# Output projection of a linear-attention + MLP block: seven block products for blocks 0 and 1 in one pair of output chunks, accumulators loaded by chunks into attention's tiles

## Chip, cores, metric

One core of one Trainium2 chip. The metric is the device time of the whole kernel in microseconds, lower is better.

## The reference: what is computed

Cut to what matters (S = 2048 tokens, D = 640 features, 32 heads of 20, MLP width 1728, all float32):

```python
xn = _layernorm(x)
out = x + attention(xn) + mlp(xn)
# attention: qkv = xn @ wqkv; phi = softmax features of q and k, per head
#            o = phi_q (phi_k^T v) / (phi_q (phi_k^T 1));  result = o @ wo
# mlp:       gelu(layernorm(xn) @ w1 + b1) @ w2 + b2
```

The change touches only the last product, `o @ wo` (2048x640 by 640x640), and what is added to it.

## The kernel before

Everything is kept transposed: features lie on the 128 partitions, tokens on the free axis. The 2048 tokens are four blocks b of 512; the 640 features are five chunks c or m of 128. A float32 matrix product is made exact enough by splitting both operands into a high part (rounded, `F32R`) and the rest, and by adding three matmuls (`mm3`, lines 69 to 72: high by high, high by low, low by high). So one output tile (128 features by 512 tokens) of the projection takes 5 chunks by 3 = 15 matmuls of 128x512.

The order of time: queries, keys and values; then the MLP of blocks 0 and 1 is done (its sums wait in DRAM as `a0` and `a1`); then the MLP of blocks 2 and 3 runs on TensorE, with attention (class `Attention`) beside it; last comes the output projection, which this case is about.

Before the projection, attention leaves its quotient in `ob`, one tile of five chunks for each block. `split` turns it into high parts `oh` (ScalarE) and low parts `ol` (VectorE) in the token order that the matmuls want. For block 3 the reciprocals `rx` come last: VectorE spreads them over partitions (`stream_shuffle`, line 1263) and GpSimd multiplies (line 1265), chunk by chunk, while the projection of the earlier blocks is already running.

The projection before:

- Blocks 0 and 1: ten calls of `column`, one for each block and output chunk m: 15 matmuls into PSUM bank 6 or 7 in turn, then VectorE adds the bank to the accumulator (line 1481) and SyncE stores the result.
- Blocks 2 and 3, output chunks 0 to 3 (two pairs, k = 0 and 1): seven block products in place of eight (Strassen-Winograd over pairs of input chunks, pairs of output chunks and the two token blocks). `product` makes 6 matmuls; `rest` adds the fifth input chunk (3 matmuls); `read` (line 1518) is VectorE adding a PSUM bank to an accumulator. Banks are named a, b and c; a bank is read in the middle and accumulated further, so the next product in it waits for that read. Output chunk 4 of both blocks is a `column` as before.
- The combined operands. Sums of the weights: loaded by `load_sums`, added on GpSimd by `add` (line 1424), split by `hi_sum` on ScalarE (line 1427) and by `lo_sum` on VectorE (line 1431). Differences of the attention outputs: `combine` on GpSimd (line 1440), `turn_hi` on ScalarE (line 1456, once into SBUF and once into a PSUM bank, bank 3 or 4 in turn), `turn_lo` on VectorE (line 1461). There are eight of these (i = 1 to 4, q = 0 and 1).

What sets the order: TensorE, VectorE, ScalarE and GpSimd run the order in which the program is written, each strictly in turn. The steps beside the matmuls are hung on ticks: `mlp.tick()` is called once per group of three matmuls in the program, and the list `steps` says at which tick each step is issued. So a step's place in VectorE's queue is fixed by hand, relative to the reads of PSUM banks that TensorE waits for. The order of SyncE's DMA queue is chosen by a scheduler.

The accumulators of blocks 0 and 1 come back from DRAM whole (1280 KB each, line 1290) into the tiles that held `ob` of these blocks.

Of the kernel before, what the change touches and what calls it, by code (L numbers as in the profile page):

```python
# [8 lines left out]
F32 = mybir.dt.float32  # L9
# [42 lines left out]
def tile_kernel(ctx: ExitStack, tc: tile.TileContext, x, xT, wkT, wqT, wv, wphi, wo, w1, b1, w2, b2,  # L52
# [1109 lines left out]
    class Attention:  # L1162

        def __init__(self, b, bank):
            self.b, self.n, self.bank = b, 0, bank
            self.ob = acc01.tile([P, KC, 512], F32, name=f"acc{b % 2}")
            self.ts = ep.tile([P, 512], F32, name="ts")
            self.t10 = ep.tile([42, 512], F32, name="t10")
            self.es = {}
# [101 lines left out]
        def split(self, c, eng):  # L1271

            b = self.b

            def tokens(ap):
                return ap.rearrange("p (q t n) -> p t q n", q=4, t=4)

            def parts(ap):
                return ap.rearrange("p (t q n) -> p t q n", q=4, t=4)

            if c == 0:
                self.oh, self.ol = (yp.tile([P, KC, 512], F32R, name=f"y{p}{b % 2}") for p in range(2))
            if c < KC:
                nc.scalar.activation(parts(self.oh[:, c, :]), tokens(self.ob[:, c, :]), AF.Copy)
            if c:
                eng.tensor_tensor(parts(self.ol[:, c - 1, :]), tokens(self.ob[:, c - 1, :]), f(parts(self.oh[:, c - 1, :])), op=ALU.subtract)
            if c == KC and b < 2:

                acc[b] = tfp.tile([P, KC, 512], F32, name=f"tf{b}")
                nc.sync.dma_start(acc[b], a_dram[b])  # L1290
# [10 lines left out]
    def first_split():  # L1301
        for c in range(KC + 1):
            at[0].split(c, nc.vector)
            if c % 2:
                yield
# [84 lines left out]

    w2t, parts = mlp.take_pair(6, True, 3)
    ws = pairs(w1t, w2t)
    for b in range(2, 4):
# [8 lines left out]
        else:  # L1402
            load_wo()
            mlp.beside = both(mlp.beside, first_split())
    finish(before)
    load_ob(1)

    sums, turned = [], {}

    def load_sums():  # L1410
        sums.append(wp.tile([P, 4, D], F32, name="w3").rearrange("p i d -> p (i d)")[:, :4 * 512])
        nc.sync.dma_start(sums[0].rearrange("p (c n) -> p c n", c=4), wo[:4 * P, :512].rearrange("(c p) n -> p c n", p=P))
        hi = wp.tile([P, 4, D], F32R, name="w1").rearrange("p i d -> p (i d)")
        lo = [bp.tile([P, 11, P], F32R, name="kvs").rearrange("p i d -> p (i d)"), rp.tile([P, 3, 2, P], F32R, name="s").rearrange("p i k n -> p (i k n)")]
        sums.extend([hi, lo])

    def lo_part(o):
        return sums[2][0][:, o:] if o < 5 * 256 else sums[2][1][:, o - 5 * 256:]

    def add(i):  # L1420

        (a11, a12), (a21, a22) = ([sums[0].rearrange("p (q r k j n) -> p q r k j n", q=2, r=2, k=2, j=2)[:, :, r, :, j] for r in range(2)] for j in range(2))
# [3 lines left out]
    def hi_sum(c):  # L1426
        nc.scalar.activation(sums[1][:, c * 512:c * 512 + 512], sums[0][:, c * 512:c * 512 + 512], AF.Copy)

    def lo_sum(o, w):
        at_ = slice(o, o + w)  # L1430
        nc.vector.tensor_tensor(lo_part(o)[:, :w], sums[0][:, at_], f(sums[1][:, at_]), op=ALU.subtract)

    def combine(i, q):

        c0, c1 = 2 * q, 2 * q + 1
        x = {(b, c): at[b].ob[:, c] for b in (2, 3) for c in (c0, c1)}
        t = {j: turned[j, q][0] for j in (1, 2, 3, 4) if (j, q) in turned}
        o = ep.tile([P, 512], F32, name="e", bufs=6) if i in (2, 3) else x[2, c0 if i == 1 else c1]
        x0, x1 = {1: lambda: (x[3, c0], x[2, c0]), 2: lambda: (x[3, c1], t[1]), 3: lambda: (x[3, c1], x[3, c0]), 4: lambda: (x[2, c1], t[2])}[i]()
        nc.gpsimd.tensor_tensor(o, x0, x1, op=ALU.subtract)  # L1440
        turned[i, q] = [o]
# [3 lines left out]
    def turn_hi(i, q):  # L1445

        src = turned[i, q][0].rearrange("p (q t n) -> p t q n", q=4, t=4)
        n = 2 * (i - 1) + q
        if n == 7:
            parts = [ep.tile([P, 512], F32, name="e", bufs=6).bitcast(F32R) for _ in range(2)]  # L1450
        else:
            m = mtile(n, F32R)
            parts = [m[:, p, :512] for p in range(2)]
# [3 lines left out]
        turned[i, q] += [bank, parts]  # L1457

    def turn_lo(i, q):
        _, bank, (hi, lo) = turned[i, q]  # L1460
# [3 lines left out]
    steps += [(12 + 2 * i, lambda i=i: add(i)) for i in range(4)]  # L1464
    steps += [(20 + c, lambda c=c: hi_sum(c)) for c in range(4)]
    steps += [(22 + n, lambda o=o, w=w: lo_sum(o, w)) for n, (o, w) in enumerate(((0, 512), (512, 512), (1024, 256), (1280, 256), (1536, 512)))]
    for n, (i, q) in enumerate((i, q) for i in (1, 2, 4, 3) for q in range(2)):
        steps += [(42 + 2 * n, lambda i=i, q=q: combine(i, q)), (45 + 2 * n, lambda i=i, q=q: turn_hi(i, q)), (46 + 2 * n, lambda i=i, q=q: turn_lo(i, q))]
    for n, t in ((1, 3), (2, 28), (3, 59)):
        steps += [(t + c, lambda n=n, c=c: at[n].split(c, nc.vector)) for c in range(KC + 1)]  # L1470
# [141 lines left out]
```

## Time and profile before

| | us |
|---|---|
| median of 3 runs | 711.22 (710.29 to 712.26) |
| the profiled execution, device time | 709.75 |
| its span, first to last instruction | 708.0 |
| PE busy / DVE / ACT / POOL in the span | 701.1 / 526.4 / 353.1 / 435.6 |
| the projection's first matmul | starts at 638.88 |
| its last matmul | starts at 704.33 |

PE is TensorE, DVE VectorE, ACT ScalarE, POOL GpSimd, SP SyncE. A row of a timeline gives the start in microseconds from the span's beginning, the time taken, the engine, the source line, the operation, written tile and read tiles, the shape, and how many instructions the row merges; a bracket at the end is the idle time before it and what ended it. A matmul row's time is its way through the array, and matmuls overlap: what one more matmul costs is the distance between two starts. In rows of grouped waits, the columns are: who waited, for whom, microseconds in total, how often, the longest.

### The profile page before, as it was taken

To read this page: it belongs to the slowest core of one execution; us is meant where nothing else is said; L and a number is where in the kernel's file an instruction comes from. 1 tells how busy PE (TensorE), PEld (TensorE's weight loads), DVE (VectorE), ACT (ScalarE), POOL (GpSimd) and SP (SyncE) were. 2 spreads that over 40 slices of the span, in tenths; PEclk is the share of its full clock that TensorE was granted. 3 is DMA by queue.
4 is the path that set the end of the run, shared out by engine and by line. 5 is a ranking of instruction groups with operands and counts; after the bars stand their busy time and mean duration, and the time that the engine had idled before them with its cause. 6 is when DMAs were issued, how large, how long until landed. Compare 5 with 4: busy or idle time off the path is not lost.

```text
span 708.0 us, 9794 instructions
## 1 busy us (share of the span) xinstructions
PE 701.1 (99%) x3369; PEld 590.3 (83%) x3369; DVE 526.4 (74%) x840; ACT 353.1 (50%) x583; POOL 435.6 (62%) x374
## 2 busy tenths in 40 slices
PE   9999999999999999999999999999999999999998
PEld 7788888888888888888888888878888878888886
DVE  7877755988745788788888878748678785696773
ACT  6434554444434545544444547457676757561250
POOL 3611314577245997898777979548688897462530
PEclk9999999999999999999999999999999999999999
DMA  9823642475621227336400708873355558537212
GB/s 328 287 74 113 190 122 98 156 263 174 219 105 74 94 75 231 86 97 200 114 0 15 177 0 316 227 215 126 109 160 172 164 166 276 216 124 262 91 60 104
DMA packets 66295, 107.61 MB, mean 152 GB/s; under 512 B 7478, under 2 KB 31830, under 8 KB 64366
## 3 DMA queue, kind: packets, MB, share of 16 engines
q1 hardware_dynamic: 65942, 106.98, 47.1%
q8 instruction: 26, 0.43, 0.2%
q14 instruction: 23, 0.19, 0.1%
q10 hardware_dynamic: 304, 0.01, 0.0%
HBM read 72.42 MB, written 34.55 MB: 151 GB/s over the span
## 4 chain that ended last, share of the span: by engine, by line
PE 93%; DVE 4%; ACT 1%; DMA 1%; issue 0%; ACTq 0%; DVEq 0%; SPq 0%
PE bank L906 28%; PE bank L70 18%; PE bank L72 18%; PE bank L71 18%; PE bank L976 3%; PE bank L646 2%; PE bank L1214 1%; PE bank L1215 1%; DVE st L138 1%; DMA e<-e 1%; PE bank L308 1%; PE bank L327 1%; PE bank L326 1%; PE bank L307 1%; PE bank L1146 1%
## 5 line engine op out<-in xcount | busy, mean ns | idle before, releaser
L906 PE MATMUL bank<-wkh,y 128*128 128x512 f32 (+1 forms) x480 | 139.6, 365 | 0.0
L64 POOL TENSOR_TENSOR w<-r,w 128x640 fp32r<-128x640 f32 x32 | 52.3, 1648 | 93.1 <-ACT w L61 57.7
L70 PE MATMUL bank<-m,w 128*128 128x512 f32 x274 | 108.0, 394 | 1.1 <-DVE acc L329 1.0
L71 PE MATMUL bank<-m,w 128*128 128x512 f32 x274 | 106.8, 390 | 0.0
L70 PE MATMUL bank<-y,w 128*128 128x512 f32 (+1 forms) x274 | 106.5, 389 | 0.0
L71 PE MATMUL bank<-y,w 128*128 128x512 f32 (+1 forms) x274 | 106.1, 387 | 0.0
L72 PE MATMUL bank<-y,w 128*128 128x512 f32 (+1 forms) x270 | 104.4, 387 | 0.0
L72 PE MATMUL bank<-m,w 128*128 128x512 f32 x262 | 102.1, 390 | 0.0
L906 PEld LDWEIGHTS bank<-wkh,y 128*128 128x128 f32 x480 | 87.6, 188 | 13.2
L906 PE MATMUL bank<-wkl,y 128*128 128x512 f32 (+1 forms) x240 | 87.4, 364 | 0.0
L942 ACT ACTIVATE m<-m,rs_all 128x1280 f32<-128x1280 f32 x32 | 43.7, 1365 | 42.9 <-POOL m L941 42.8
L70 PEld LDWEIGHTS bank<-m,w 128*128 128x128 f32 x274 | 51.5, 188 | 12.4 <-DVE acc L329 1.4
L70 PEld LDWEIGHTS bank<-y,w 128*128 128x128 f32 x274 | 51.5, 188 | 10.8 <-issue 0.4
L71 PEld LDWEIGHTS bank<-y,w 128*128 128x128 f32 x274 | 51.5, 188 | 10.5 <-DMA y<-t 0.4
L71 PEld LDWEIGHTS bank<-m,w 128*128 128x128 f32 x274 | 51.5, 188 | 10.4 <-DVE m L461 0.2
L72 PEld LDWEIGHTS bank<-y,w 128*128 128x128 f32 x270 | 50.8, 188 | 10.3
L944 DVE TENSOR_REDUCE sm<-m 128x64 f32<-128x1280 f32 x32 | 47.4, 1482 | 14.9 <-ACT m L942 14.8
L72 PEld LDWEIGHTS bank<-m,w 128*128 128x128 f32 x262 | 49.2, 188 | 10.3
L906 PE MATMUL bank<-w,y 128*128 128x512 f32 x240 | 57.4, 391 | 0.0
L941 POOL TENSOR_TENSOR m<-m,mx 128x640 f32<-128x640 f32 (+2 forms) x48 | 44.4, 938 | 19.3 <-DVE mx L930 19.3
L331 DVE TENSOR_TENSOR acc<-bank,acc 128x512 f32<-128x512 f32 x70 | 47.0, 684 | 11.0 <-PE bank L72 6.1
L64 DVE TENSOR_TENSOR m<-m,m 128x512 fp32r<-128x512 f32 (+1 forms) x34 | 27.9, 828 | 36.0 <-ACT m L61 36.0
(216 smaller groups left out, 1516.7 us busy)
## 6 DMA issues: line engine op xcount, KB each, us to landing
r<-in_w SPq DMA_DIRECT2D x52, 320.0 KB
e<-e SPq DMA_DIRECT2D x40, 256.0 KB
e<-acc SPq DMA_DIRECT2D x52, 160.0 KB
acc<-in_xT SPq DMA_DIRECT2D x4, 1280.0 KB
t<-t SPq DMA_DIRECT2D x8, 512.0 KB
tf<-t SPq DMA_DIRECT2D x2, 1536.0 KB
xb<-in_x SPq DMA_DIRECT2D x8, 320.0 KB
t<-in_x SPq DMA_DIRECT2D x8, 320.0 KB
```

The source lines that it names most:

```text
L64: eng.tensor_tensor(lo, src, f(hi), op=ALU.subtract)
L70: nc.tensor.matmul(ps, lh, rh, start=first, stop=False, **kw)
L71: nc.tensor.matmul(ps, lh, rl, start=False, stop=False, **kw)
L72: nc.tensor.matmul(ps, ll, rh, start=False, stop=last, **kw)
L138: nc.vector.bn_stats(st[:, i, h, :], xb[:, h * 320:(h + 1) * 320])
L331: nc.vector.tensor_tensor(acc[b][:, m, :], pw, acc[b][:, m, :], op=ALU.add)
L646: nc.tensor.matmul(ps[:, u * nh * DF:(u + 1) * nh * DF], raw[:nh * DH, u * P:(u + 1) * P], wpt[:nh * DH, g, :nh, 1:], start=True, stop=True)
L906: nc.tensor.matmul(ps, lh[:, kc, c], rh[:, kc], start=n == 0, stop=n == 3 * KC - 1)
L941: subs[n, t] = nc.gpsimd.tensor_tensor(ep[:, s], a, b, op=ALU.subtract)
L942: exps[n, t] = nc.scalar.activation(e, e, AF.Exp, scale=rs_all[:, t:t + 1])
L944: nc.vector.tensor_reduce(sm, e.rearrange("p s (h f) -> p (s h) f", f=DH), axis=AX, op=ALU.add)
L976: nc.tensor.matmul(kvp[g // 2][:, (g % 2) * 240:(g % 2) * 240 + 240].rearrange("p (s f) -> p s f", s=4), v[:, g * VS:(g + 1) * VS], ft[:, ...
```

## The change

In the projection of blocks 0 and 1 the output chunks 0, 1 and 4 stay `column`s (six of them). Chunks 2 and 3 (the pair k = 1) are now made with the seven block products too: `opened(0, 1)` and `closed(0, 1)`, which are the old loop bodies made into functions, and which are called one straight after the other. For blocks 2 and 3 the order stays: both `opened`, the column, both `closed`.

What comes with it:

- Eight more combined operands for blocks 0 and 1: `combine`, `turn_hi`, `turn_lo` with b0 = 0. They overwrite `ob` of these blocks. Those with i = 1 are written over chunks 0 and 2 of `oh` and `ol` of block 1.
- `ob` must live on, so the accumulators of blocks 0 and 1 come one chunk at a time (256 KB each) into attention's `e` tiles, `ts`, `t10`, `ph` and a part of `w3` (`load_a`, `load_sums`). They are queued before the projection begins.
- `split` is cut in two steps, and blocks 2 and 3 put their parts into the tiles of blocks 0 and 1, so each chunk's split waits until the last product that reads the old chunk is through.
- `lo_sum` is done for the pair k = 1 first (ticks 20 to 26), and for k = 0 late (ticks 56 to 62).
- The last operand's parts go into a tile `rx`.

```diff
-    for b in range(2):
-        for m in range(KC):
-            column(b, m, [6 + (b + m) % 2])
+    for n, (b, m) in enumerate((b, m) for b in range(2) for m in (0, 1, 4)):
+        column(b, m, [6 + n % 2])
+    opened(0, 1)
+    closed(0, 1)
     for k in range(2):
-        place("a", k, k)
...
+        opened(2, k)
     column(2, 4, [2])
     for k in range(2):
...
+        closed(2, k)
```

The two functions, which before stood in the loops with block 2 and 3 written in:

```diff
+    def opened(b0, k):
+        place("a", k, k)
+        product("a", k, "a11", "b11", b0, True)
+        read("a", k, 0, b0, False)
+        place("c", k, (2, 5)[k])
+        product("c", k, "a12", "b21", b0, True)
+        rest("c", k, 0, b0)
+        read("c", k, 0, b0)
+
+    def closed(b0, k):
+        place("b", k, (5, 2)[k])
+        product("b", k, "s1", "t1", b0, True)
+        read("b", k, 1, b0 + 1, False)
+        product("a", k, "s2", "t2", b0)
+        read("a", k, 0, b0 + 1, False)
+        place("c", k, (2, 5)[k])
+        product("c", k, "a22", "t4", b0, True)
+        rest("c", k, 1, b0)
+        read("c", k, 1, b0, False)
+        product("a", k, "s3", "t3", b0)
+        read("a", k, 1, b0)
+        product("b", k, "s4", "b22", b0)
+        rest("b", k, 0, b0 + 1)
+        read("b", k, 0, b0 + 1)
+        rest("a", k, 1, b0 + 1)
+        read("a", k, 1, b0 + 1)
```

Loads, splits and the table of steps:

```diff
+    def load_a():
+        for b, m in ((0, 0), (0, 1), (0, 4), (1, 0), (0, 2), (0, 3)):
+            accs[b, m] = ep.tile([P, 512], F32, name="e", bufs=6)
+        for m, n in ((1, "ts"), (2, "t10"), (3, "ph")):
+            accs[1, m] = ep.tile([P, 512], F32, name=n)
+        for b, m in ((0, 0), (0, 1), (0, 4), (1, 0), (1, 1), (0, 2), (1, 2), (0, 3), (1, 3)):
+            nc.sync.dma_start(accs[b, m], a_dram[b][:, m])
...
+            if (c, part) == (0, 0):
+                self.oh, self.ol = (at[self.b - 2].oh, at[self.b - 2].ol) if self.b > 1 else \
+                    (yp.tile([P, KC, 512], F32R, name=f"y{p}{self.b % 2}") for p in range(2))
...
-    steps += [(22 + n, lambda o=o, w=w: lo_sum(o, w)) for n, (o, w) in enumerate(((0, 512), (512, 512), (1024, 256), (1280, 256), (1536, 512)))]
-    for n, (i, q) in enumerate((i, q) for i in (1, 2, 4, 3) for q in range(2)):
-        steps += [(42 + 2 * n, lambda i=i, q=q: combine(i, q)), (45 + 2 * n, lambda i=i, q=q: turn_hi(i, q)), (46 + 2 * n, lambda i=i, q=q: turn_lo(i, q))]
+    steps += [((56, 20)[k] + 2 * c, lambda c=c, k=k: lo_sum(c, k)) for c in range(4) for k in range(2)]
+    for b0, t0, order in ((0, 17, (1, 3, 2, 4)), (2, 41, (1, 2, 4, 3))):
...
+            t = t0 + 2 * n
+            h = 30 + 2 * q if (b0, i) == (0, 1) else t + 3
...
+    for n, c, t in [(1, c, 3 + c) for c in range(KC)] + [(2, c, t) for c, t in ((0, 31), (2, 32), (1, 34), (3, 35), (4, 42))] + [(3, c, 57 + c) for c in range(KC)]:
```

How this moves instructions. First VectorE, at the place where TensorE makes its first block products (blocks 2 and 3 before; blocks 0 and 1 now). In the names, `tf1`, `acc2`, `acc3` and `e_5997` are accumulators, a `bank` is a PSUM bank with its physical number first, `m` and `y11_6077` hold the parts of combined operands (banks 3 and 4 are their copies), and `y10_6018` holds the low parts of block 2. Before:

```order
L1481 TENSOR_TENSOR tf1_6091<-bank7_6273,tf1_6091 128x512
L1461 TENSOR_TENSOR m3_6311<-bank4_6312,m3_6311 128x512
L1518 TENSOR_TENSOR acc2_4122<-bank0_6307,acc2_4122 128x512
L1461 TENSOR_TENSOR m6_6325<-bank3_6326,m6_6325 128x512
L1518 TENSOR_TENSOR acc2_4122<-bank2_6321,acc2_4122 128x512
L1461 TENSOR_TENSOR e_6339<-bank4_6340,e_6338 128x512
```

And now, from the read of the last column of block 1 on:

```order
L1503 TENSOR_TENSOR w3_6064<-bank7_6196,w3_6064 128x512
L1478 TENSOR_TENSOR y11_6077<-bank4_6226,y01_6076 128x512
L1478 TENSOR_TENSOR m1_6229<-bank3_6230,m1_6229 128x512
L1281 TENSOR_TENSOR y10_6018<-acc0_5165,y00_6017 128x512
L1536 TENSOR_TENSOR e_5997<-bank1_6237,e_5997 128x512
L1478 TENSOR_TENSOR y11_6077<-bank4_6248,y01_6076 128x512
L1478 TENSOR_TENSOR m4_6251<-bank3_6252,m4_6251 128x512
L1281 TENSOR_TENSOR y10_6018<-acc0_5165,y00_6017 128x512
L1263 STREAM_SHUFFLE rx_4376<-rx_4376 128x512
L1478 TENSOR_TENSOR m5_6270<-bank4_6271,m5_6270 128x512
L1281 TENSOR_TENSOR y10_6018<-acc0_5165,y00_6017 128x512
L1536 TENSOR_TENSOR e_5997<-bank5_6258,e_5997 128x512
```

From the last column's read to the read of bank c (bank 2 before, bank 5 now) there stood three other instructions on VectorE; now there are ten, of which three are block 2's low parts and one is a shuffle for block 3.

Second TensorE, where bank c is used for the second time. Before, in `closed(2, 0)`, bank 2 stands here (the column of block 2 used it last):

```order
L72 MATMUL bank0_6307<-m3_6311,kvs_6051 128x512
L70 MATMUL bank2_6423<-m6_6325,w2_5985 128x512
L71 MATMUL bank2_6423<-m6_6325,w2_5985 128x512
L72 MATMUL bank2_6423<-m6_6325,w0_5989 128x512
L70 MATMUL bank2_6423<-e_6338,w2_5985 128x512
```

And now, in `closed(0, 1)`, where the names say bank 5 again, 12 matmuls after the last one into `bank5_6258`:

```order
L72 MATMUL bank1_6237<-m1_6229,s_6069 128x512
L70 MATMUL bank5_6303<-m4_6251,w2_5985 128x512
L71 MATMUL bank5_6303<-m4_6251,w2_5985 128x512
L72 MATMUL bank5_6303<-m4_6251,w0_5989 128x512
L70 MATMUL bank5_6303<-m5_6270,w2_5985 128x512
```

Before, bank 2 had been read long ahead, since both `opened` and a column lay between; now two products of six matmuls lie between.

Third VectorE again, just before the first `closed` of blocks 2 and 3. Before, block 3's low parts (`y11_6373`) and reads stood here, the sums' low parts (`kvs`) having been made long ahead:

```order
L1286 TENSOR_TENSOR y11_6373<-acc1_5547,y01_6372 128x512
L1518 TENSOR_TENSOR acc2_4122<-bank5_6360,acc2_4122 128x512
L1286 TENSOR_TENSOR y11_6373<-acc1_5547,y01_6372 128x512 x4
L1481 TENSOR_TENSOR acc2_4122<-bank2_6383,acc2_4122 128x512
L1518 TENSOR_TENSOR acc3_4123<-bank5_6408,acc3_4123 128x512
```

Now the four low parts for k = 0 are among them:

```order
L1441 TENSOR_TENSOR kvs_6068<-w3_6064,w1_6066 128x256
L1478 TENSOR_TENSOR m4_6416<-bank3_6417,m4_6416 128x512
L1441 TENSOR_TENSOR kvs_6068<-w3_6064,w1_6066 128x256
L1281 TENSOR_TENSOR y11_6077<-acc1_5547,y01_6076 128x512
L1536 TENSOR_TENSOR acc2_4122<-bank5_6411,acc2_4122 128x512
L1478 TENSOR_TENSOR m5_6429<-bank4_6430,m5_6429 128x512
L1281 TENSOR_TENSOR y11_6077<-acc1_5547,y01_6076 128x512
L1441 TENSOR_TENSOR kvs_6068<-w3_6064,w1_6066 128x256
L1281 TENSOR_TENSOR y11_6077<-acc1_5547,y01_6076 128x512 x2
L1441 TENSOR_TENSOR kvs_6068<-w3_6064,w1_6066 128x256
```

They are read by the first product of `closed(2, 0)`, so they have moved from well before the block products to right ahead of their use.

150 lines of the change are left out of this document (70 added, 80 removed).

## Prediction

> **What bounds the kernel now.** I read the head of the page, then who waits for whom on TensorE, then the stages of the projection as windows, and last the timelines of that stretch.
>
> ```profile
> PE 701.1 (99%) x3369; PEld 590.3 (83%) x3369; DVE 526.4 (74%) x840; ACT 353.1 (50%) x583; POOL 435.6 (62%) x374
> PE bank L579 <- POOL m L577: 1.3, 1, 1.3
> PE bank L70 <- DVE acc L329: 1.0, 1, 1.0
> PE bank L1214 <- DVE acc L1228: 0.6, 1, 0.6
> ```
>
> TensorE sets the time: it is busy 99% of the span, and after its start the longest wait that it had for anyone is 1.0 us. None of the three lies in the projection. Fewer matmuls shorten the kernel, and each wait put into TensorE's path lengthens it.
>
> ```profile
> 638.80:656.00 17.20, 17.20 (x77) 14.22 (x77) 9.54 (x16) 2.31 (x4) 5.16 (x4) 1.00 0.79 277
> 656.00:673.00 17.00, 17.00 (x77) 14.08 (x76) 13.02 (x23) 5.47 (x10) 11.02 (x9) 1.00 0.24 87
> 673.00:683.20 10.20, 10.20 (x47) 8.45 (x46) 9.07 (x16) 8.86 (x17) 5.73 (x5) 1.00 0.19 69
> ```
>
> The columns after the window are its length, then busy time and count of PE, weight loads, DVE, ACT, POOL, then the clock and the DMA share. TensorE has no gap, but VectorE is busy for 13.02 of 17.00 us beside block 1's columns and 9.07 of 10.20 beside the first block products: there it has 4.0 and 1.1 us to spare. The change puts its new work there.
>
> ```profile
> 642.37 0.39 PE L70 MATMUL bank<-y,w 128*128 128x512 f32 x1
> 645.77 0.39 PE L70 MATMUL bank<-y,w 128*128 128x512 f32 x1
> ```
>
> These are the starts of two columns: 15 matmuls in 3.40 us, 0.227 us each.
>
> **What is removed.** One pair of output chunks for two blocks was four columns, 4 x 15 = 60 matmuls; now it is seven products of 6 and four rests of 3, 54. Six matmuls fewer, 6 x 0.227 = 1.36 us, all on the path.
>
> **What is added, and where it hides.** ScalarE gets 16 copies (0.63 and 0.58 us by the rows below), GpSimd eight subtractions. Both have room in 638.8 to 656 (2.31 and 5.16 busy of 17.20), so their time costs nothing as long as GpSimd can start early. VectorE gets eight low parts, four more reads and three more, smaller, low parts of sums.
>
> ```profile
> 668.73 0.63 ACT L1456 ACTIVATE m<-acc 128x512 fp32r<-128x512 f32 x1 [9.84 <-POOL acc L1440]
> 669.27 0.58 ACT L1456 ACTIVATE bank<-acc 128x512 f32<-128x512 f32 x1
> 675.51 0.68 DVE L1518 TENSOR_TENSOR acc<-bank,acc 128x512 f32<-128x512 f32 x1
> 678.02 0.68 DVE L1518 TENSOR_TENSOR acc<-bank,acc 128x512 f32<-128x512 f32 x1
> 653.38 1.62 DVE L1431 TENSOR_TENSOR kvs<-w,w 128x512 fp32r<-128x512 f32 x3
> 654.92 0.42 DVE L1431 TENSOR_TENSOR s<-w,w 128x256 fp32r<-128x256 f32 x1
> 657.39 0.74 DVE L1263 STREAM_SHUFFLE rx<-rx 128x512 f32<-128x512 f32 x1
> 658.02 2.37 DVE L1286 TENSOR_TENSOR y<-acc,y 128x512 fp32r<-128x512 f32 x2
> 660.32 0.72 DVE L1263 STREAM_SHUFFLE rx<-rx 128x512 f32<-128x512 f32 x1
> 661.54 1.43 DVE L1286 TENSOR_TENSOR y<-acc,y 128x512 fp32r<-128x512 f32 x1
> 681.76 2.49 DVE L1286 TENSOR_TENSOR y<-acc,y 128x512 fp32r<-128x512 f32 x4
> 658.21 1.63 POOL L1265 TENSOR_TENSOR acc<-acc,rx 128x512 f32<-128x512 f32 x1 [6.18 <-DVE rx L1263]
> 661.12 1.29 POOL L1265 TENSOR_TENSOR acc<-acc,rx 128x512 f32<-128x512 f32 x1 [1.28 <-DVE rx L1263]
> ```
>
> Prices on VectorE, from start to next start: an instruction that reads a PSUM bank 0.62 (four from 675.51 to 678.02); a shuffle 0.63 (657.39 to 658.02); a low part of a 256-wide sum 0.34 (654.92 - 653.38 - 2 x 0.60). A split from SBUF takes 0.60 alone (2.49 for four). Beside GpSimd it takes longer: that of 661.54 ended at 662.97, 0.56 behind GpSimd's end at 662.41, as if it had waited until GpSimd let go; the two of 658.02 lasted until the shuffle at 660.32, 2.30 for both. I take 1.35 where GpSimd is running, and for the worst 1.70 (2.30 - 0.60).
>
> [...]
>
> **First wait: bank 5.** After the last column of block 1, TensorE makes a (6 matmuls), c with its rest (9), b (6) and a again (6): 27 x 0.227 = 6.12 us. Then it wants bank 5 again for the second c, and has to wait until VectorE has read the first c out of it. VectorE's twelve instructions from the column's read to that read stand in the order shown: eight read PSUM (8 x 0.62 = 4.96), one shuffle (0.63), three splits of block 2. GpSimd works beside them (its combines for blocks 0 and 1, and the multiplications for block 3, which need those shuffles), so I take two splits at 1.35 and one at 0.60: 3.30. Sum 8.89. The column's result comes 0.39 us after its last matmul's start, 0.16 behind the next start, and the last read ends 0.07 later than its distance; with two hand-overs of 0.03 (the row of 704.33 below ends at 704.61, and VectorE starts at 704.64) that is 9.18. TensorE waits 9.18 - 6.12 = 3.1 us, part of it perhaps one product earlier, where b's second half wants the low part of t1 from the same queue. Ends: no split held up, 8.89 - 1.50 = 7.39 and a wait of 1.6; all three at 1.70, 4.9. That it is nil is the first rival below.
>
> ```profile
> 704.33 0.28 PE L72 MATMUL bank<-y,r 128*128 128x256 f32 x1
> 704.64 0.42 DVE L1481 TENSOR_TENSOR acc<-bank,acc 128x256 f32<-128x256 f32 x1 [1.37 <-PE bank L72]
> ```
>
> **Second wait: bank 1.** Nine matmuls on (2.04 us) the third product into a wants its second read done. Behind the read of c, VectorE has a split, a shuffle, the read of b, a shuffle and then the read of a: 0.60 + 0.63 + 0.62 + 0.63 + 0.62 = 3.10. TensorE waits 1.1 us more; 1.8 if the split is held up.
>
> **Third wait: the late sums.** From there TensorE has 68 matmuls to the sixth of `closed(2, 0)`, 15.4 us, and that one reads the last low part for k = 0. VectorE has 25 instructions ahead of it: 16 that read PSUM (9.92), five splits (3.0, and 0.75 if one is held up) and four low parts of sums (1.36), 15.0 in all. It also idles while ScalarE waits for GpSimd's differences; before, that was 2.5 us in this stage.
>
> ```profile
> DVE m L1461 <- ACT bank L1456: 2.5, 3, 1.3
> ```
>
> With 2.0 of it the wait is 15.0 + 2.0 - 15.4 = 1.6 us, spread over reads and the sums; ends 0 and 3.0. The end of the kernel behind it, two half columns and their stores, is unchanged.
>
> **Loads.** The chunks of the accumulators go out in SP's queue beside the last MLP matmuls, 2304 KB while the MLP's own loads are over; the high and low weights of the projection stand between them and wait for nothing later than they did. I cost them at nothing: the first column's matmuls and reads cover them, and an accumulator is needed only at a column's end. What gets better is hidden too: VectorE waited 1.77 us for the whole accumulator at 643.75 without TensorE noticing.
>
> ```profile
> 638.21 0.32 SPq L1290 DMA_DIRECT2D tf<-a  x1
> 643.75 0.69 DVE L1481 TENSOR_TENSOR tf<-bank,tf 128x512 f32<-128x512 f32 x1 [1.77 <-DMA tf<-a]
> 638.95 0.39 SPq L1412 DMA_DIRECT2D w<-in_wo  x1
> 646.64 5.39 POOL L1424 TENSOR_TENSOR w<-w 128x512 f32<-128x512 f32 x4 [12.90 <-DMA w<-in_wo]
> ```
>
> GpSimd's start hangs on the weights of the last two rows. They landed at 646.64, behind 1280 KB of accumulator; now 256 KB stand ahead, and I estimate 644.2: 2304 KB took 8.4 us from the accumulator's issue at 638.21; with some 2 us of it before anything flows, 1280 KB take 5.6 us from an issue at about 638.6.
>
> **Sum.** -1.36 + 3.1 + 1.1 + 1.6 = +4.4 us. The profiled execution, 709.75 with a span of 708.0, would become 714.2. It lies below all three timed runs, so I add the difference to their median: 711.22 + 4.4 = 715.6.
>
> **Rivals.** *VectorE keeps up* (8%): then only the six matmuls are left, 711.22 - 1.36 = 709.9. It decides at the read of bank 5: the twelve instructions would have to fit in some 5.8 us, 0.49 each, and no such row above is under 0.60. For it speaks only that I place the queue's start at the column's end.
>
> *GpSimd starts late* (12%): if the weights land at 646.64 as before, GpSimd's adds (5.39) and its seven first differences end 2.4 us later. I see no slack there, since ScalarE, and VectorE behind it, wait for each of them; so up to 2.4 more, 718.0.
>
> *The clock falls* (4%): the kernel's first 18 matmuls took 7.21 us, 0.39 each without the last one's 0.16 of latency; as many at that pace after a long wait cost 18 x 0.165 = 3.0 more, 718.6. Against it: the clock column reads 1.00 in every window above. [...]
>
> ```profile
> 1.31 7.21 PE L579 MATMUL bank<-m 128*128 128x512 f32 x18 [1.31 <-POOL m L577]
> ```
>
> That the matmuls are not saved can be excluded: the built order has six fewer.
>
> **How the numbers follow.** The forecast has 76%. Its ends: 1.6 + 1.1 + 0 - 1.36 = +1.3, 712.6; and 4.9 + 1.8 + 3.0 - 1.36 = +8.3, 719.6, which needs every split held up. I give 712.4 to 718.7, which leaves out the first rival, most of such a pile-up and a little of the third. About 0.3% (2.1 us) is what a measurement of this kernel can tell from no change: slower begins at 713.4, faster at 709.1. Slower: 70 of the forecast's 76, and the second and third rival, 86%. The same: the forecast's low end and most of the first rival, 11%. Faster: 3%.
>
> **What would show it.** In the profile after: TensorE waiting for VectorE's adds (line 1536) at the first line-70 matmul of the second c, some 27 matmuls behind the last column, for 2 to 3 us, and again nine matmuls on; VectorE without a gap between; the low part of the late sums (line 1441) or a read ahead of it as a third releaser; splits beside GpSimd's rows ending half a microsecond behind them. I am wrong if TensorE runs through this stage without a gap, or if its wait there is for a DMA or for GpSimd.

## The result, and the profile after

The changed kernel takes 715.06 us (median of six runs, 713.73 to 717.1) against 711.17 before (six runs, 710.2 to 712.3): 1.0061 times as long, with a 95% interval of 1.0044 to 1.0078. That is 3.9 us more; 4.4 were forecast. The profiled execution took 714.46 us with a span of 712.6, 4.6 more than the span before.

The head of the page, and then all waits of TensorE from 636 us on:

```profile
PE 702.2 (99%) x3363; PEld 589.8 (83%) x3363; DVE 536.7 (75%) x855; ACT 361.8 (51%) x599; POOL 446.9 (63%) x382
```

```profile
PE bank L70 <- DVE e L1536: 2.3, 1, 2.3
PE bank L71 <- DVE y L1478: 0.8, 1, 0.8
PE bank L72 <- DVE kvs L1441: 0.3, 1, 0.3
```

Six matmuls are gone (3369 to 3363), and TensorE, which waited for nobody in the projection before, now waits three times, each time for VectorE. The three waits are 3.4 us, and the matmuls saved are 1.36: that alone would be 2.0 us more, not 4.6. The rest is in no wait. Single matmuls show it:

```profile
638.37 0.47 PE L70 MATMUL bank<-y,w 128*128 128x512 f32 x1
...
658.65 0.39 PE L72 MATMUL bank<-y,r 128*128 128x512 f32 x1
...
662.96 0.39 PE L70 MATMUL bank<-y,w 128*128 128x512 f32 x1
664.10 0.50 PE L71 MATMUL bank<-y,w 128*128 128x512 f32 x1 [0.75 <-DVE y L1478]
...
665.82 0.39 PE L72 MATMUL bank<-m,s 128*128 128x512 f32 x1
668.54 0.47 PE L70 MATMUL bank<-m,w 128*128 128x512 f32 x1 [2.34 <-DVE e L1536]
...
670.07 0.63 PE L72 MATMUL bank<-m,w 128*128 128x512 f32 x1
670.49 0.63 PE L70 MATMUL bank<-y,r 128*128 128x512 f32 x1
...
671.77 0.63 PE L70 MATMUL bank<-m,w 128*128 128x512 f32 x1
...
688.36 0.50 PE L72 MATMUL bank<-m,kvs 128*128 128x512 f32 x1 [0.32 <-DVE kvs L1441]
...
708.55 0.28 PE L72 MATMUL bank<-y,r 128*128 128x256 f32 x1
```

Behind the wait of 2.34 us the distance from start to start is not 0.227 but 0.42 us. The windows say why:

```profile
666.00:669.40 3.40, 1.06 (x5) 0.76 (x5) 3.40 (x6) 0.00 (x0) 1.25 (x1) 1.00 0.04 15
669.40:672.80 3.40, 3.40 (x10) 2.57 (x9) 2.84 (x7) 0.79 (x2) 3.07 (x3) 0.50 0.17 62
672.80:676.00 3.20, 3.20 (x16) 2.61 (x15) 2.44 (x3) 1.62 (x4) 3.20 (x3) 1.00 0.16 58
```

From 669.4 to 672.8 us, 3.4 us that begin 0.9 behind the wait's end, TensorE was granted half its clock (0.50). Summing each start-to-start distance less its 0.227 gives the whole account of the projection: 1.0 at the first wait, 2.6 at the second, 1.6 of half clock, 0.7 at the late sums and a read shortly before, 0.2 of small change; 6.1 in all. From its first matmul (638.37) to its last (708.55) the projection takes 70.18 us, before 65.45 (638.88 to 704.33): 6.1 less 1.36 is the difference of 4.7.

VectorE on the same stretch, the whole projection before and after in one window each, and then its rows ahead of the wait of 2.34:

```profile
638.80:704.70 65.90, 65.80 (x304) 54.92 (x303) 41.95 (x70) 16.64 (x30) 21.91 (x17) 1.00 0.38 137
```

```profile
638.30:709.00 70.70, 67.12 (x298) 54.53 (x297) 52.08 (x85) 25.16 (x46) 33.22 (x25) 0.98 0.26 94
```

```profile
659.78 0.67 DVE L1503 TENSOR_TENSOR w<-bank,w 128x512 f32<-128x512 f32 x1
...
661.57 1.28 DVE L1281 TENSOR_TENSOR y<-acc,y 128x512 fp32r<-128x512 f32 x1
662.77 0.68 DVE L1536 TENSOR_TENSOR e<-bank,e 128x512 f32<-128x512 f32 x1
...
664.57 0.67 DVE L1281 TENSOR_TENSOR y<-acc,y 128x512 fp32r<-128x512 f32 x1
...
666.40 1.40 DVE L1281 TENSOR_TENSOR y<-acc,y 128x512 fp32r<-128x512 f32 x1
667.72 0.68 DVE L1536 TENSOR_TENSOR e<-bank,e 128x512 f32<-128x512 f32 x1
668.32 0.67 DVE L1281 TENSOR_TENSOR y<-acc,y 128x512 fp32r<-128x512 f32 x1
...
670.77 0.68 DVE L1536 TENSOR_TENSOR t<-bank,t 128x512 f32<-128x512 f32 x1
...
687.89 0.41 DVE L1441 TENSOR_TENSOR kvs<-w,w 128x256 fp32r<-128x256 f32 x1
```

VectorE has 10.1 us more to do for the 1.36 that TensorE is spared. It goes from row to row without a gap, and TensorE resumes at 668.54 when the read of 667.72 is through.

### The profile page after: what moved, and what is told of

It is laid out like the page before. It is cut to its first block, busy times and chain, and to the rows that moved or that the text cites. A ratio compares the mean times of both kernels' runs of the same rounds, so it can differ in the third digit from the quotient of the medians.

```text
span 712.6 us, 9846 instructions
## 1 busy us (share of the span) xinstructions
PE 702.2 (99%) x3363; PEld 589.8 (83%) x3363; DVE 536.7 (75%) x855; ACT 361.8 (51%) x599; POOL 446.9 (63%) x382
## 4 chain that ended last, share of the span: by engine, by line
PE 87%; DVE 6%; DMA 2%; POOL 1%; issue 1%; ACT 1%; SPq 1%; POOLq 0%; ACTq 0%; DVEq 0%
PE bank L906 28%; PE bank L70 16%; PE bank L72 16%; PE bank L71 16%; PE bank L976 3%; PE bank L646 2%; PE bank L1214 1%; PE bank L1215 1%; DMA e<-e 1%; DMA xb<-in_x 1%; DVE st L138 1%; PE bank L326 1%; PE bank L327 1%; PE bank L308 1%; PE bank L307 1%
## 5 line engine op out<-in xcount | busy, mean ns | idle before, releaser
L70 PE MATMUL bank<-m,w 128*128 128x512 f32 x280 | 110.6, 395 | 3.5 <-DVE e L1536 2.3
L71 PE MATMUL bank<-m,w 128*128 128x512 f32 x280 | 109.5, 391 | 0.0
L71 PE MATMUL bank<-y,w 128*128 128x512 f32 (+1 forms) x266 | 102.9, 387 | 0.8 <-DVE y L1478 0.8
L70 PE MATMUL bank<-y,w 128*128 128x512 f32 (+1 forms) x266 | 103.4, 389 | 0.0
L72 PE MATMUL bank<-m,w 128*128 128x512 f32 x264 | 103.1, 390 | 0.0
L72 PE MATMUL bank<-y,w 128*128 128x512 f32 (+1 forms) x258 | 99.6, 386 | 0.0
L70 PEld LDWEIGHTS bank<-m,w 128*128 128x128 f32 x280 | 52.8, 189 | 15.4 <-issue 2.7
L71 PEld LDWEIGHTS bank<-m,w 128*128 128x128 f32 x280 | 52.8, 188 | 10.6 <-DVE m L461 0.2
L71 PEld LDWEIGHTS bank<-y,w 128*128 128x128 f32 x266 | 50.0, 188 | 11.0 <-DVE y L1478 1.2
L70 PEld LDWEIGHTS bank<-y,w 128*128 128x128 f32 x266 | 50.0, 188 | 10.8 <-issue 0.4
L72 PEld LDWEIGHTS bank<-m,w 128*128 128x128 f32 x264 | 49.7, 188 | 10.5
L72 PEld LDWEIGHTS bank<-y,w 128*128 128x128 f32 x258 | 48.5, 188 | 9.9
```

The costliest lines, as they stand in the source:

```text
L70: nc.tensor.matmul(ps, lh, rh, start=first, stop=False, **kw)
L71: nc.tensor.matmul(ps, lh, rl, start=False, stop=False, **kw)
L72: nc.tensor.matmul(ps, ll, rh, start=False, stop=last, **kw)
```

## The experiments

My theory was that the length of VectorE's queue up to each read sets when TensorE goes on, and that the bank is only where this shows. The rivals: the use of bank 5 twice in a row; the half clock; the chunked loads and the late sums; the place of a few instructions in the queue, rather than their number.

All runs at a glance. The ratio is to the kernel before on the same chip, with its 95% interval; "projection" is the profiled execution, from the first to the last matmul's start; "lowest clock" is that granted in the projection of the same execution.

| | ratio | projection, us | lowest clock |
|---|---|---|---|
| before | 1 | 65.45 | 1.00 |
| changed | 1.0061 [1.0044, 1.0078] | 70.18 | 0.50 |
| second c in bank 7 | 1.0076 [1.0063, 1.0088] | 69.77 | 0.50 |
| wait filled, 10 matmuls | 1.0066 [1.0054, 1.0079] | 69.84 | 1.00 |
| wait filled, 4 matmuls | 1.0076 [1.0062, 1.0090] | 69.86 | 1.00 |
| four low parts left out | 1.0024 [1.0014, 1.0034] | 66.58 | 1.00 |
| four low parts later | 1.0053 [1.0033, 1.0074] | 70.75 | 0.50 |
| ten columns | 1.0013 [1.0002, 1.0024] | 66.08 | 1.00 |
| ten columns, early sums | 0.9997 [0.9986, 1.0008] | 65.47 | 1.00 |
| differences first | 1.0049 [1.0033, 1.0065] | 67.94 | 1.00 |
| differences first, q = 1 ahead | 1.0073 [1.0061, 1.0086] | 68.62 | 1.00 |
| steps spread | 1.0057 [1.0040, 1.0075] | 67.82 | 1.00 |
| two low parts on GpSimd | 1.0069 [1.0056, 1.0082] | 67.68 | 1.00 |

**Is it the bank?** In `closed`:

```diff
-        place("c", k, (2, 5)[k])
+        place("c", k, (2, 5)[k] if b0 else 7)
         product("c", k, "a22", "t4", b0, True)
```

> The second c of closed(0, 1) goes into bank 7, which nobody uses any more, so that it need not wait for VectorE's read of bank 5. If VectorE's queue sets the pace (my theory), the wait only moves: TensorE runs the second c from about 666.1 on, nine matmuls to 668.1, and the third product into bank 1 then waits for VectorE's read of that bank, which ended at 670.2 in the trace of the changed kernel: a wait of about 2.1 us there. The end is between 713.5 (clock stays at 1.00) and 715.1 (clock falls to 0.50 behind the new wait as it did behind the old one). If the use of bank 5 twice is itself the cost, the 2.3 us wait and the 1.6 us of half clock behind it are gone: about 711.1.

TensorE's row at the third product into bank 1, and the clock behind it:

```profile
672.56 0.80 PE L70 MATMUL bank<-m,w 128*128 128x512 f32 x1 [3.24 <-DVE t L1536]
```

```profile
672.60:675.40 2.80, 2.80 (x7) 2.23 (x8) 1.25 (x2) 1.12 (x2) 2.80 (x3) 0.50 0.00 0
```

The wait only moved nine matmuls on, to the read of bank 1, and the clock fell just the same: 0.76% over the kernel before where the changed kernel has 0.61%. That bank 5 is the cause is excluded. The wait is 3.2 us where I expected 2.1, and the time is above the expected range. I had taken 670.2 for the end of the read of bank 1 in the changed kernel's trace; that is the end of the read before it (669.55 + 0.67), and bank 1's own ends at 670.77 + 0.68 = 671.45.

**Is it the half clock?** Matmuls whose results nobody reads, ahead of the second c; ten in one run, four in another:

```diff
+        if b0 == 0:
+            spare = banks.tile([P, 512], F32, name="bank6")
+            for n in range(10):
+                nc.tensor.matmul(spare, wol[0][4][:, :P], at[0].oh[:, 4], start=n == 0, stop=n == 9)
         place("c", k, (2, 5)[k])
```

> Ten matmuls of 128x512 into bank 6, whose results nobody reads, stand ahead of the second c of closed(0, 1): 10 x 0.227 = 2.27 us of work in the wait of 2.34. If the granted clock of 0.50 behind the wait (669.4 to 672.8 in the trace of the changed kernel) comes from TensorE standing idle, it stays at 1.00 now, the nine matmuls of the second c and those behind take 0.227 each, and the kernel with ten more matmuls is 1.6 us shorter than the changed kernel: 713.5. The read of bank 1 (ended at 670.2) is then just in time for the third product at 670.6. If the clock falls for another reason, or if VectorE's queue makes up the difference in a later wait, the time stays at 715.1. If the wait was not really for VectorE, the fillers lengthen the kernel by up to 2.3: 717.3.

With ten, TensorE's rows and a window behind them:

```profile
666.50 2.43 PE L1558 MATMUL bank<-y,r 128*128 128x512 f32 x10
669.03 0.47 PE L70 MATMUL bank<-m,w 128*128 128x512 f32 x1
...
671.99 0.50 PE L70 MATMUL bank<-m,w 128*128 128x512 f32 x1 [0.67 <-DVE t L1536]
```

```profile
669.00:672.00 3.00, 2.30 (x10) 1.62 (x10) 3.00 (x8) 0.63 (x1) 1.78 (x2) 1.00 0.23 87
```

The clock stays at 1.00 where it was 0.50 in the changed kernel, so it was TensorE's idleness that had lowered it. But the 1.6 us that I expected from this do not come: the ratio is 1.0066 and the projection 69.84 us. Now TensorE is early at bank 1 and waits there (0.67; its read ends later than the 670.2 that I had taken from the trace here too), and again at 678.33 (0.61, for the read of another bank). The half clock had cost next to nothing by itself here (the projections differ by 0.3 us); it had filled time that VectorE took anyway. My expectation of 713.5 fell, and its second alternative, that VectorE's queue makes up the difference, holds.

> Four unread matmuls (0.9 us) instead of ten ahead of the second c of closed(0, 1): TensorE's wait there is 1.4 us instead of 2.3. The clock stayed at 1.00 in the runs with single waits of up to 1.3 us and fell in those with 2.0 to 3.2. If the length of the wait decides, it stays at 1.00 here, and the wait for bank 1 of some 0.7 us shows nine matmuls on, as with ten fillers. If the clock falls here too, a wait of 1.4 us behind one of 0.4 to 0.8 is enough. Either way VectorE's queue sets the time: 0.55% to 0.7% over the kernel before.

With four, TensorE's wait at bank 5 and a window behind it:

```profile
669.92 0.47 PE L70 MATMUL bank<-m,w 128*128 128x512 f32 x1 [1.47 <-DVE e L1536]
```

```profile
670.00:672.00 2.00, 2.00 (x9) 1.50 (x9) 2.00 (x6) 0.00 (x0) 0.89 (x1) 1.00 0.35 131
```

A wait of 1.47 us is left, and the clock stays at 1.00; the wait at bank 1 is 0.67 again. The projection takes 69.86 us; the ratio of 1.0076 lies above the 0.55% to 0.7% that I expected, with an interval that reaches down to 0.62%.

**Is it VectorE's queue?** The low parts of block 2's chunks 0 to 3 left out (first), or only put later (second):

```diff
-        steps += [(t + part, ...) for part in range(2)]
+        steps += [(t + part, ...) for part in range(2) if (n, part) != (2, 1) or c == 4]
```

```diff
+        steps += [({0: 37, 2: 38, 1: 41, 3: 42}.get(c, t + 1) if (n, part) == (2, 1) else t + part, ...) for part in range(2)]
```

> VectorE's low parts of block 2's chunks 0 to 3 (line 1281) are left out; so block 2's low parts are missing from the result. Three of the four stand ahead of the read of bank 5, with 1.20, 0.60 and 1.32 us of VectorE's queue in the trace of the changed kernel, 3.1 in all. If the order and length of VectorE's queue set the wait, the two waits of 0.75 and 2.34 shrink to under 0.8 together, the clock does not fall, and the time is 715.1 - 3.0 - 1.6 = 710.5, about what the removed matmuls would have given. If VectorE is held there by ScalarE's copies or GpSimd's differences, which this edit leaves as they are, the wait stays over 1.5 us and the time over 712.5.

```profile
PE bank L70 <- DVE t L1536: 0.6, 1, 0.6
PE bank L70 <- DVE e L1536: 0.4, 1, 0.4
PE bank L72 <- DVE kvs L1441: 0.3, 1, 0.3
```

Four instructions less on VectorE, and the projection is 3.6 us shorter (66.58). The wait for t1's low part is gone, that for bank 5 is 0.4, and the clock stays at 1.00. The time is 2.0 us over the kernel before; I had expected about as much as before. Of this the projection shows 1.1: the waits at 676.3 (0.6) and at the late sums (0.3) are still there. Of the other 0.9, some 0.4 lies behind the last matmul (see the end of the next section); the rest is not explained.

> Nothing is left out: the low parts of block 2's chunks 0 to 3 only stand later in VectorE's queue, behind the read of bank 5 (steps 37, 38, 41, 42 in place of 32, 33, 35, 36). If the place of a few instructions ahead of one read is the cause, this gains what leaving them out gained, some 2 us on the changed kernel. If the amount of work in VectorE's queue is the cause (my theory now), the wait for bank 5 shrinks to about 0.8 us and the clock stays at 1.00, but the low parts (four, 0.6 each alone, 1.3 where they fall beside a GpSimd difference) hold up the reads of bank 1 behind them: new waits of 2 to 4 us there, and no more than 1 us gained: 0.4% to 0.7% over the kernel before.

VectorE's low parts that now stand ahead of the last read of bank 1 but one (676.69), and TensorE's wait for it:

```profile
671.59 3.49 DVE L1281 TENSOR_TENSOR y<-acc,y 128x512 fp32r<-128x512 f32 x2
...
675.61 1.16 DVE L1281 TENSOR_TENSOR y<-acc,y 128x512 fp32r<-128x512 f32 x1
676.69 0.68 DVE L1536 TENSOR_TENSOR e<-bank,e 128x512 f32<-128x512 f32 x1
```

```profile
677.42 0.50 PE L70 MATMUL bank<-y,r 128*128 128x512 f32 x1 [2.00 <-DVE e L1536]
```

The same instructions put later gain nothing that can be measured (1.0053): the waits become 0.37 at bank 5, then 1.75 and 2.00 at bank 1, and the clock falls behind the last. It is the number of instructions, not their place. (The profile is of the longest of this kernel's six runs, 717.15 us, and of the only one with a mean clock of 0.998; the other five have 1.000, so the clock fell in this one alone, and its projection of 70.75 us is at the upper end.)

**The loads and the late sums.** The changed kernel with ten columns and without the eight operands for blocks 0 and 1; in the second run the sums' low parts for k = 0 are early too:

```diff
-    for n, (b, m) in enumerate((b, m) for b in range(2) for m in (0, 1, 4)):
+    for n, (b, m) in enumerate((b, m) for b in range(2) for m in range(KC)):
         column(b, m, [6 + n % 2])
-    opened(0, 1)
-    closed(0, 1)
...
-    for b0, t0, order in ((0, 17, (1, 3, 2, 4)), (2, 41, (1, 2, 4, 3))):
+    for b0, t0, order in ((2, 41, (1, 2, 4, 3)),):
```

```diff
-    steps += [((56, 20)[k] + 2 * c, lambda c=c, k=k: lo_sum(c, k)) ...]
+    steps += [((21, 20)[k] + 2 * c, lambda c=c, k=k: lo_sum(c, k)) ...]
```

> The changed kernel with its chunked accumulators, its cut splits and its late sums, but with ten columns for blocks 0 and 1 and without the eight operands for them. If the loads, the places in memory and the order of the steps cost nothing (as I summed it), it takes what the kernel before takes, 711.2, or up to 0.5 more for the late sums; TensorE then waits nowhere in the projection for more than 0.5 us. If the loads or the late sums are where the time comes from, it shows 1 to 3.5 us of the loss: 712.2 to 714.7.

> The run with ten columns again, with the low parts of the sums for k = 0 early too (steps 21 to 27 instead of 56 to 62). Its wait of 0.39 us for a read (684.6) stood behind such low parts; if the late sums were all of its loss, the projection takes from first to last matmul what it took before, 65.45 us, and the time is that of the kernel before within 0.1%. If the chunked loads cost something by themselves, 0.5 us or more is left.

With the late sums the projection takes 66.08 us and has one wait:

```profile
685.01 0.47 PE L70 MATMUL bank<-m,w 128*128 128x512 f32 x1 [0.39 <-DVE acc L1536]
```

With early sums it takes 65.47, and TensorE waits nowhere; the ratio is 0.9997. So the chunked loads and the new places in memory cost nothing, and the late sums 0.6 us by themselves.

**Can VectorE's idle time before 655 take the work?** GpSimd's differences for blocks 0 and 1 ahead of its sums of weights:

```diff
-    steps += [(8 + 2 * i, lambda i=i: add(i)) for i in range(4)]
-    steps += [(18 + c, lambda c=c: hi_sum(c)) for c in range(4)]
-    steps += [((56, 20)[k] + 2 * c, lambda c=c, k=k: lo_sum(c, k)) ...]
+    steps += [(15 + i, lambda i=i: add(i)) for i in range(4)]
+    steps += [(23 + c, lambda c=c: hi_sum(c)) for c in range(4)]
+    steps += [((56 + 2 * c, 27 + c)[k], lambda c=c, k=k: lo_sum(c, k)) ...]
...
-            t = t0 + 2 * n
+            t = t0 + 2 * n if b0 else min(6 + 2 * n, 7 + n)
```

> GpSimd makes the eight differences for blocks 0 and 1 ahead of the four sums of weights, which wait for a load until 644.8; ScalarE's and VectorE's parts follow. VectorE stands idle for some 6 us between 642 and 655.8 (2.71, 1.82, 0.91, 0.60 in front of the columns' reads); six of the eight low parts (3.6 us) can go there, and the four low parts of sums (0.33 each) come behind them. By my theory the stretch ahead of the read of bank 5 is 2.3 us shorter: the wait there falls from 2.34 to under 0.7, the clock stays at 1.00, and a wait of about 1.5 is left at bank 1: 2 to 3 us less than the changed kernel, 0.2% to 0.35% over the kernel before. If GpSimd can't start earlier because block 1's quotient is late, nothing moves: 0.6%.

In part. The projection is 67.94 us, 2.2 shorter than the changed kernel's, with waits of 0.3 and 1.2 in place of 2.3 and without a fall of the clock. But half of it is lost ahead of the first column. GpSimd, VectorE and TensorE there:

```profile
635.81 1.30 POOL L1453 TENSOR_TENSOR tf<-tf,tf 128x512 f32<-128x512 f32 x1 [1.31 <-DVE y L1281]
638.34 1.29 POOL L1453 TENSOR_TENSOR tf<-tf,tf 128x512 f32<-128x512 f32 x1 [1.23 <-DVE y L1281]
```

```profile
636.25 2.01 DVE L1281 TENSOR_TENSOR y<-tf,y 128x512 fp32r<-128x512 f32 x2
...
638.78 1.99 DVE L1281 TENSOR_TENSOR y<-tf,y 128x512 fp32r<-128x512 f32 x2
640.70 1.87 DVE L331 TENSOR_TENSOR acc<-bank,acc 128x512 f32<-128x512 f32 x3
```

```profile
641.48 0.47 PE L70 MATMUL bank<-y,w 128*128 128x512 f32 x1 [1.13 <-issue]
```

Two splits take 2.0 us beside a difference (1.28 alone), so the last reads of the MLP's banks (line 331) come late, and with them the first column: it starts 0.78 us after those three reads begin, here and in the kernel before (638.10 and 638.88). Two further runs bear on this: one tries to mend it and begins with q = 1, the other spreads all steps of the table by hand.

> The run with the differences first, but beginning with q = 1, which needs block 1's chunks 2 and 3, so that GpSimd can't begin at 635.8 beside the last MLP matmuls. There, two differences held up VectorE's splits (2.01 and 1.99 us for two, against 1.28 alone) and with them the reads of the MLP's banks, and TensorE waited 1.13 us for its first column. If that is so, the 1.1 us go and the projection stays at about 68 us from first to last matmul: about 0.35% over the kernel before, against 0.49%. If the 1.13 us had another cause, the time stays.

```diff
-        for n, (i, q) in enumerate((i, q) for i in order for q in range(2)):
-            t = t0 + 2 * n
+        for n, (i, q) in enumerate((i, q) for i in order for q in ((0, 1) if b0 else (1, 0))):
+            t = t0 + 2 * n if b0 else 8 + n
```

The sums of weights stand as in the run before. The same three engines again:

```profile
636.32 2.97 POOL L1453 TENSOR_TENSOR tf<-tf,tf 128x512 f32<-128x512 f32 x2 [3.12 <-DVE y L1281]
```

```profile
636.76 3.08 DVE L1281 TENSOR_TENSOR y<-tf,y 128x512 fp32r<-128x512 f32 x2
639.77 1.87 DVE L331 TENSOR_TENSOR acc<-bank,acc 128x512 f32<-128x512 f32 x3
```

```profile
640.54 0.47 PE L70 MATMUL bank<-y,w 128*128 128x512 f32 x1 [1.76 <-issue]
```

A miss: differences with i = 1 overwrite block 0's quotient only, so they need block 0's splits alone, and both still begin at 636.32, now in one piece. Two splits take 3.08, the wait grows to 1.76, and the ratio to 1.0073. The fix failed, and the cause showed itself more clearly.

> The changed kernel with the same matmuls in the same order, and with its steps spread so that VectorE has as little as possible in front of each read: differences ahead of the sums of weights, block 2's low parts spread over the stretch to its first product, the late sums a little earlier. By my theory VectorE's work, 3 us shorter than its matmuls need in this stretch, then fits almost: waits of TensorE of 1 to 2 us in all, no fall of the clock, and with six matmuls fewer (1.36) a time within 0.1% of the kernel before. If bank 5 or the loads were the cause, it stays 0.5% slower. Faster by over 0.1% would mean that VectorE can be brought to keep up entirely.

```diff
-    steps += [(8 + 2 * i, lambda i=i: add(i)) for i in range(4)]
+    steps += [([15, 15, 15, 17][i], lambda i=i: add(i)) for i in range(4)]
...
+    for b0, ts, order in ((0, [[8, 30, 31], [11, 32, 33], [11, 12, 17], ...
```

Another miss: 1.0057. The same 1.13 us is lost ahead of the first column, and 3.7 us in the projection (67.82 where the matmuls alone give 65.45 - 1.36 = 64.09), the largest part (1.0) a wait for t1's low part at 666.6. Same number of matmuls, same number of instructions on VectorE, another order: no gain that can be measured against the changed kernel. My expectation had put a time like this down to bank 5 or the loads; the run with the second bank and those with ten columns exclude both. What it does show is that I could not spread the steps so that VectorE keeps up.

> In addition, GpSimd makes the low parts of block 2's chunks 0 and 2 (1.3 us each there) in its idle time between block 3's multiplications, the low parts of the late sums come six steps earlier, and the c of the first two block products of blocks 2 and 3 goes to banks 6 and 7. VectorE has 1.5 to 2 us less ahead of the read of bank 1. By my theory the waits in the projection fall from 3.9 to about 2.6 us, and the time is 0.15% to 0.3% over the kernel before: work taken off VectorE shows in the time, one for one. If GpSimd's differences become the bound instead, waits for VectorE behind ScalarE's copies at 676 to 688 take up what is gained, and it stays at 0.35% to 0.5%.

```diff
-                nc.vector.tensor_tensor(lo, src, f(hi), op=ALU.subtract)
+                (nc.gpsimd if self.b == 2 and c in (0, 2) else nc.vector).tensor_tensor(lo, src, f(hi), op=ALU.subtract)
...
-        place("c", k, (2, 5)[k])
+        place("c", k, (6, 7)[k] if b0 else 5)
```

This run also holds the edit of the run with q = 1 ahead, and its loss of 1.8 us, and it makes the late sums' low parts six ticks earlier. Against that run the projection is 0.9 us shorter (67.68), somewhat less than the 1.3 expected; in the whole time (1.0069 against 1.0073) it can't be told, and the 0.15% to 0.3% expected are missed. The 0.9 us belong to all three edits together. VectorE has two instructions less than in that run (853 against 855), but is busy for 538.5 us where it was 538.9: most of the time that they took is back in others. No version beat the kernel before; the nearest is the one that makes ten columns.

## Why the prediction was right

*What is removed.* 297 matmuls from 303 in the projection, 1.36 us; as forecast.

*First wait, 3.1 us at bank 5, part of it perhaps one product earlier.* It was 3.6: 1.0 where b's second half wants t1's low part, 2.6 at bank 5. The twelve instructions took 668.32 - 659.78 = 8.54 us (8.89 forecast), and the three splits 1.20, 0.60 and 1.32, 3.12 in all (3.30 forecast: two of three beside GpSimd). What I had too small is the start: the column's result was there at 658.65 + 0.39 = 659.04, and VectorE, behind already, read it at 659.78.

*Second wait, 1.1 us at bank 1.* It did not come; 1.6 us of half clock stood in its place. The rival of the falling clock (4%) named this: I left it at 4% because I took a wait of 3.1 split by a product for too short, which no run had shown; here 2.34 behind 0.75 was enough. It put its price on top of the waits (718.6), and that is where it fails: while TensorE runs slowly (0.42 us from start to start), VectorE catches up. The filled waits show it: with the clock at 1.00 the second wait is back, with 0.67 us. Among the six timed runs of the changed kernel the two with the highest mean clock (0.999 and 1.000, the others 0.998) are the longest, 716.22 and 717.1; with the low parts later the one run in which the clock fell is the longest, so single runs do not settle it.

*Third wait, 1.6 us at the late sums.* 0.7. VectorE needed from the end of the read of bank 1 (671.45) to the last needed low part (688.30) 16.9 us, 17.0 forecast, and was idle for 1.8 of it, 2.0 forecast; but TensorE started 0.3 behind the end of that read, and lost half a microsecond of the 1.6 after it. The size was off because I treated the three waits as independent, while they are parts of one lag.

*The sum.* VectorE's way from the column's read to the last low part was forecast as 8.89 + 3.10 + 17.0 = 29.0 us and was 688.30 - 659.78 = 28.5. TensorE, from the column's last matmul (658.65) to the one that reads that low part (688.36), took 29.7 where its 105 matmuls need 23.8. So 5.9 of the 6.1 us stand on this way: they are VectorE's queue, 28.5 - 23.8 = 4.7, and its start, 1.1 behind that matmul; how they are shared out among waits and clock does not matter to the sum. So the misses of the single terms (the third 0.9 below its forecast, the first and the clock in place of the second each 0.5 above) offset each other because they share one lag. By chance alone, two smaller misses offset each other: the queue was 0.5 shorter than forecast, and its start 0.7 later. About 1.3 us of the queue is the time by which two of the three splits lasted longer beside GpSimd (1.20 and 1.32 against 0.60); no run takes GpSimd's work away to show it alone.

*Loads.* Nothing, as forecast, shown by the run with ten columns and early sums. GpSimd started on the landed weights at 644.80, 1.8 us before its old time; 644.2 was my estimate. The 2 us or so before anything flows, which it rests on, are shown only roughly: in the profile before, DMA moves nothing from the issue at 638.21 to 639.1 (0.9 us), 0.26 MB from there to 640.5, and 437 GB/s in the 1.5 us after that. In the changed kernel:

```profile
644.80 5.38 POOL L1434 TENSOR_TENSOR w<-w 128x512 f32<-128x512 f32 x4 [11.80 <-DMA w<-in_wo]
```

So the rival of the late GpSimd did not come about, and *VectorE keeps up* is excluded: not even with four low parts left out does it keep up.

*The end.* The prediction put it as unchanged, and it is not. From the last matmul's start to the end of the span the kernel before takes 707.97 - 704.33 = 3.64 us, the changed one 712.64 - 708.55 = 4.09. The last stores land 2.6 behind that matmul in both; what comes later is GpSimd's closing instructions. The runs with ten columns have 3.64 and 3.65, all others 3.94 to 4.09. Why is not shown. So the 4.6 us between the two spans are 4.7 of projection and 0.4 of end, less the 0.5 by which the first column starts earlier.

Two things stay open. The medians differ by 3.9 us, the two profiled projections by 4.7. And in six of the experiments the whole time is 0.5 to 1.2 us more over the kernel before than the projection and the wait ahead of it account for; 0.3 to 0.45 of it is the longer end, and one profile of each is too little to tell what else varies.

## What to carry to other kernels

Price a saved matmul against the instructions that it costs the engine behind it: here 0.227 us each against 10.1 us of VectorE's work for six. In this kernel VectorE's queue was the bound: another bank (1.0076), a filled wait (1.0066) or a later place (1.0053) moved the wait and kept the time (1.0061); fewer instructions shortened it (2.0 us over the kernel before in place of 3.9, with four left out). Work brought into time in which its inputs are ready shortened the projection by 2.2 us in one profile; in the whole time, with 1.0049 against 1.0061, that gain can't be told. Add up the slow engine's whole way to the last point that waits for it, rather than wait by wait.

## What the runs showed of the hardware

Waits of TensorE lowered its clock to 0.50. It fell with single waits of 2.34 us (with 0.75 some 2 us before), 3.24 us, and 2.00 us (with 1.75 some 3.7 us before), and not with 1.47, 1.19 or 1.76; each time for about 3.4 us, and then it was 1.00 again. In the 3.4 us ahead of the fall in the changed kernel TensorE was busy for 1.06 (the first of the three windows above).

The length of a single wait is not what these traces go by. With the second bank the clock fell at 672.13, 0.4 us before the wait was over (672.56); in the changed kernel at 669.41, 0.9 behind the wait's end. In the kernel before it fell at 707.12, 2.5 us behind the last matmul's end, while in the changed kernel it is still 1.00 when the span ends, 3.8 us behind the last matmul's. The clock records of these two traces change at distances that are whole multiples of 3.413 us: full clock lasts 662.19 us up to the fall in the changed kernel (194 times), 0.50 then 3.41 (once), and full clock again 40.96 (12 times, past the span's end); in the kernel before full clock lasts 699.73 (205 times). Cut along each run's own stretches of 3.41, those in front of the falls have 1.07 us of busy TensorE (changed kernel), 0.60 (second bank), 1.41 (low parts later) and 0.90 (the end of the kernel before). Those that hold the longest waits without a fall have 1.64 (two low parts on GpSimd, a wait of 1.77) and 1.95 (four fillers, a wait of 1.47); the last whole one of the changed kernel, 706.96 to 710.37, has 1.87. The two nearest to each other, the first with a fall behind it:

```profile
674.52:677.93 3.41, 1.41 (x6) 0.86 (x6) 3.41 (x6) 1.75 (x3) 3.41 (x4) 1.00 0.00 0
```

```profile
639.14:642.55 3.41, 1.64 (x7) 1.24 (x7) 3.41 (x5) 0.00 (x0) 0.71 (x1) 1.00 0.63 166
```

So in these runs the clock fell behind a stretch with at most 1.41 us of work and stayed at 1.00 behind those with 1.64 or more, and how the idle time lay across two stretches counted beside its length: 2.5 us without a matmul at the end of the kernel before saw a fall, 3.8 at the end of the changed one none. It also fits that the clock fell in one of six runs of the kernel with the low parts later (a mean of 0.998) and not in the others (1.000); only the one with the fall has a trace.

Two of VectorE's subtractions of two SBUF operands ended 0.55 and 0.56 us behind a running GpSimd instruction's end, with starts 0.56 and 0.42 behind its start: those of 661.57 and 666.40 at 662.85 and 667.80, GpSimd's at 662.30 and 667.24.

```profile
661.01 1.29 POOL L1453 TENSOR_TENSOR tf<-tf,tf 128x512 f32<-128x512 f32 x1
665.98 1.26 POOL L1265 TENSOR_TENSOR acc<-acc,rx 128x512 f32<-128x512 f32 x1 [1.99 <-DVE rx L1263]
```

The rows look as if VectorE's instruction waited the other's out and then took some 0.55 us; alone one takes 0.60 from start to start (664.57 to 665.17).
